# Carrying the odd head quads' outputs into the even quads' empty rows: an output projection of five matmuls per tile instead of eight

## The chip, the cores and the metric

The kernel runs on one core of one Trainium2 chip. The metric is the device time of one execution in microseconds (us). The profile is of one execution and reads the busy and waiting time of each engine: TensorE (PE, with its weight loads as PEld), VectorE (DVE), ScalarE (ACT), GpSimd (POOL) and SyncE (SP), whose queue here issues nearly all DMAs.

## The reference

A transformer block with adaptive layer norm, for 2048 tokens of width D = 512, in bfloat16. Cut to what matters:

```python
mod = silu(c) @ w_mod                      # six vectors of 512: sa, ca, ga, sb, cb, gb
h = layernorm(x) * (1 + ca) + sa
q, k, v = split(h @ wqkv)                  # 32 heads of 16 columns
o = softmax(q k^T / 4) v                   # per head, all 2048 keys
x = x + ga * (o @ wo)                      # the output projection that is changed
h = layernorm(x) * (1 + cb) + sb
x = x + gb * ((gelu(h @ w_gate) * (h @ w_up)) @ w_down)   # inner width 1792
```

The scores are 32 x 2048 x 2048 numbers, and each of them needs an exponential. Head h owns columns 16h to 16h + 15 of o, and so rows 16h to 16h + 15 of wo.

## The kernel before, in words

**Units and steps.** The queries are cut into six sets (`SETS`): three of 512, one of 256 and two of 128. A *unit* is one set with one *quad* of four heads. Eight quads cover the 32 heads: quad qd holds heads 8(qd//2) + 2j + (qd mod 2) for j = 0 to 3, so an even quad has the even heads of a group of eight and the following odd quad the odd ones. For the first four quads, the two sets of 128 are run as one unit of 256. A *step* of the main loop (`stream`, lines 1202 to 1453) is one group of score matmuls into three PSUM banks (ps_sc), and one ScalarE instruction that takes the exponentials of them. There are two such groups of banks, so the matmuls of a step wait until ScalarE is done with the step before the last. ScalarE writes 1536 columns (three banks) or 1024. Where it writes 1024, VectorE makes the third bank's exponentials by an integer trick: one tensor_scalar per bank out of PSUM (L338, into dreg or mreg), and after four of them four shifted copies (mreg<-dreg, mreg<-mreg).

**Output of a unit.** The value matmuls of a quad write four blocks of 17 rows into ps_pv, at partitions 0, 32, 64 and 96: sixteen rows of output and, as the seventeenth, the softmax's denominators. `unit_end` (lines 1506 to 1545) copies that to SBUF (osb), and sends the denominators through a chain of DMAs on SP's queue: osb to DRAM (`scr_den`), back as 128 partitions (`den`), a reciprocal on VectorE, to DRAM again (`scr_rec`), and four broadcasting loads into `rb`. Then `fin2` multiplies osb by rb on VectorE and writes `onorm[:, qd]`. Quads 6 and 7 of the last two sets take a shorter way (`near_end`, lines 934 to 949): a selecting matmul (osb,self) spreads the denominators and VectorE takes reciprocals of 128 x 128. In `onorm[:, qd]` sixteen of every 32 rows carry outputs; the others are zero or meet zero rows of the projection's weights.

**Output projection.** `side_wo` (lines 951 to 966) makes, for each tile of 128 queries, eight matmuls over 128 rows and 512 columns, one per quad (`wo_mm`). In the main loop each is issued as four instructions of 32 output rows (`mm` with `split`, lines 304 to 314), which run side by side. I call such a four a *group*. The weights `wo` are eight tiles, each zeroed first, with sixteen of every 32 rows loaded (`side_wo_load`) and multiplied by ga (`scale_wo`). The last set's projection is `wo_last`, with the eighth matmul in `tail_end`.

**What sets the order.** Nothing is scheduled while the kernel runs: a recorder writes each engine's list of instructions when the program is built. It holds a model of each engine's time and of DMA latencies, and at each point chooses between the next step's score matmuls, value matmuls, side work (the projections and the feed-forward part of an earlier set, `side_ffn`, given out by a credit against due positions in `plan`), and idle matmuls (`xs,ident`) that it adds where the last 3413 ns held fewer than `FILL` columns (`short`). VectorE, SP and some ScalarE work stands in a list of tasks, taken by `urgency` (lines 1083 to 1093). Each engine then runs its own list in order and waits on semaphores, so a late operand holds up everything behind it on that engine. After the last step, `tail` orders what is left: the last set's projection, its layer norm and feed-forward part.

Line 313 is `mm`'s matmul, 326 `act`, 330 `tt`, 338 `ts`, 343 `stt`, 347 `copy`, 350 `recip`, 376 the DMA, and `ps_mi` the PSUM bank of the side work.

Of the kernel before, what the change touches and what calls it, by code (L numbers as in the profile page):

```python
# [7 lines left out]
BF16 = mybir.dt.bfloat16  # L8
# [5 lines left out]
P = 128  # L14
S_TOK = 2048
D = 512
# [16 lines left out]
BCOL = (0, 0, 0, 0, 0, 128)  # L33
QS = 4
CH = 3
SC = 2 * CH
# [382 lines left out]
class _Kernel(_Recorder):  # L419
# [12 lines left out]
    def alloc(self):  # L432
# [31 lines left out]
        self.vs = sb("vs", [P, len(SHIFT), NKT - T0, H * VW], BF16)  # L464
        self.wo = sb("wo", [P, 8, D], BF16)
        self.E = sb("E", [P, NSL, 512], BF16)
# [368 lines left out]
    def side_wo_load(self):  # L835

        if not self.dry:
            self.task([lambda qd=qd: self.memset("dve", self.wo[:, qd, :], 0.0) for qd in range(8)]
                      + [lambda: self.memset("dve", self.self32[:, :], 0.0)], "wo0")
        yield from self.until("wo0")  # L840
        selv = self.self32[:, :].rearrange("p (a b) -> p a b", b=32)
        self.affine_select(selv, [[-32, 4], [0, 32]], ALU.not_equal, 1.0, -16, 1)
        for j in range(4):
            for ee in range(2):
                src = self.A_wo.rearrange("(a j e r) n -> j e r a n", j=4, e=2, r=DH)[j, ee]
                self.dma("sp", self.wo[32 * j:32 * j + DH, ee:8:2, :], src, "wo%d" % (2 * j + ee))
        yield END
# [22 lines left out]
    def scale_wo(self):  # L870

        if not self.dry:
            self.task([lambda qd=qd: self.tt("dve", self.wo[:, qd, :], self.wo[:, qd, :], self.ga[:, :], ALU.mult)
                       for qd in range(8)], "wo", self.after(["modB"]))
        return
        yield
# [3 lines left out]

    def wo_mm(self, bank, gi, tl, qd, first=True):
        c = OCOL[gi] + P * tl
        self.mm(bank, self.onorm[:, qd, c:c + P], self.wo[:, qd, :], start=first and qd == 0, stop=(qd == 7))

# [66 lines left out]
    def side_wo(self, gi):  # L951
        q0, W = SETS[gi]
        n = W // P
        tiles = [q0 // P + i for i in range(n)]
        mi = self.mi[:, :]
        for i in range(n):
            for qd in range(8):
                yield from self.until(("onorm", gi, qd))
                yield 512, lambda i=i, qd=qd: self.wo_mm(mi, gi, i, qd)
            self.wo_fin(mi, tiles[i])  # L960
            if not self.dry:
                self.task([lambda t=tiles[i]: self.ln_stat(t)], ("st2", tiles[i]))
# [120 lines left out]
    def urgency(self, tk):  # L1083

        if tk[1] is not None and tk[1][0] in ("rec", "onorm", "stats", "rstd") or tk[1] in ((("ln2", len(SETS) - 1, h) for h in range(2))):
            return -3
        if tk[1] is not None and tk[1][0] == "shift" and self.plain[tk[1][1]] <= LATE:
            return -2
        if tk[1] is None or tk[1][0] in ("st2", "ln2", "den"):
            return -1  # L1090
        if tk[1] is None or tk[1][0] != "shift":
            return 1
        return 0 if self.plain[tk[1][1]] <= URGENT else 2
# [412 lines left out]
    def unit_end(self, u, acc):  # L1506
# [25 lines left out]
        def fin2():  # L1532
            c = OCOL[sets[0]]
            self.tt("dve", self.onorm[:, qd, c:c + W], osb, rb, ALU.mult)
            if self.probing is None:
                self.live.pop(u)
                for k in sets:
                    self.done(("onorm", k, qd))
# [5 lines left out]
        self.task(steps, ("den", u))  # L1544
        self.task([fin2], None, free)

# [42 lines left out]
    def wo_last(self, k):  # L1589

        yield from self.until("last")
        yield from self.until("wo")
        yield 512, lambda: self.mm(self.spare[0], self.ident[:, :], self.xs[:, SETS[k][0] // P, :], start=True, stop=False)
        for qd in range(7):
            yield from self.until(("onorm", k, qd))
            yield 512, lambda qd=qd: self.wo_mm(self.spare[0], k, 0, qd, False)
        if not self.dry:
            self.done("wo_last")
        yield END

    def tail_end(self, k):
# [8 lines left out]
        yield from self.until(("onorm", k, 7))  # L1610
        yield lambda: self.wo_mm(bank, k, 0, 7, False)
        halves = [slice(0, D // 2), slice(D // 2, D)]
# [143 lines left out]
```

## Time and profile before

| what | before |
|---|---|
| median of 3 runs (range) | 859.36 us (859.06 to 859.92) |
| the profiled execution's own time | 860.08 us |
| its span, first to last instruction | 858.3 us |
| ScalarE busy | 831.8 us (97%) |
| TensorE busy | 797.3 us (93%) |
| VectorE busy | 700.3 us (82%) |
| projection matmuls in the main loop (ps_mi<-wo,onorm) | 480 instructions, 37.8 us busy |
| multiplications that write onorm | 44 |
| DMAs issued by SP | 401 |
| idle matmuls (xs,ident of 512 columns) | 396 instructions, 99 groups |

The busy time of an engine is the time in which at least one of its instructions ran. Instructions of one engine overlap, so the mean of one is longer than the distance from one start to the next. A line of waits names the engine that was idle, its tile and line, and what ended its idle time, with the sum, the number and the longest. In a line of the timeline the first number is the start, the second the length of a run of equal instructions, and a bracket gives the idle time just before and what ended it.

### The profile page before, as it was taken

The numbers are of one execution on the slowest core, as the hardware profiler recorded it, in microseconds if no ns is written. First come the engines' busy times: TensorE is split into PE (matmuls) and PEld (weight loads), VectorE is DVE, ScalarE is ACT, GpSimd is POOL, SyncE is SP. The second block draws the span as 40 slices with busy tenths as digits, with TensorE's granted clock in tenths as the row PEclk, the third lists the DMA queues.
The fourth block names the chain that finished last, engine by engine and source line by source line (L and its number), as shares of the span: only waits on it lengthen the run. The fifth ranks groups of instructions, "written<-read, shape, count | busy, mean of one in ns | idle before, by whom it ended". The sixth has DMA issues, their size and how long they took to land.

```text
span 858.3 us, 27911 instructions
## 1 busy us (share of the span) xinstructions
PE 797.3 (93%) x12580; PEld 288.0 (34%) x12582; DVE 700.3 (82%) x1351; ACT 831.8 (97%) x747; POOL 4.5 (1%) x12
## 2 busy tenths in 40 slices
PE   7889999999999899899999999999998999998998
PEld 3334332322222222222222222222343323345566
DVE  7865989989889989988898988989987764687575
ACT  6999999999999999999999999999999999999992
POOL 1000000000000000000000000000000000000000
PEclk9999999999999999999999999999999999999999
DMA  9000000000003111210002112120133222500000
GB/s 311 10 26 18 2 9 9 10 9 9 10 4 93 44 45 33 58 33 19 11 15 82 42 36 58 34 58 9 46 104 112 62 78 60 153 10 11 19 7 14
DMA packets 64233, 38.08 MB, mean 44 GB/s; under 512 B 17745, under 2 KB 61970, under 8 KB 64114
## 3 DMA queue, kind: packets, MB, share of 16 engines
q1 hardware_dynamic: 63056, 35.65, 14.7%
q8 instruction: 98, 1.61, 0.8%
q10 hardware_dynamic: 1058, 0.66, 0.3%
q14 instruction: 21, 0.17, 0.1%
HBM read 33.68 MB, written 2.61 MB: 42 GB/s over the span
## 4 chain that ended last, share of the span: by engine, by line
ACT 74%; PE 16%; DVE 7%; DMA 1%; issue 1%; SPq 0%; ACTq 0%; DVEq 0%
ACT E L326 72%; PE ps_mi L313 6%; PE ps_sc L313 6%; PE ps_pv L313 3%; ACT wreg L326 2%; DVE mreg L338 1%; DMA mreg<-in_w_mod_dram 1%; DVE st L366 1%; DVE wreg L343 1%; DVE hreg L338 1%; DVE wreg L347 1%; SPq L376 0%; DVE dreg L338 0%; DVE nwt L330 0%; DMA rb<-scr_rec 0%
## 5 line engine op out<-in xcount | busy, mean ns | idle before, releaser
L326 ACT ACTIVATE E<-ps_sc 128x1536 bf16<-128x1536 f32 (+2 forms) x698 | 804.1, 1339 | 11.6 <-PE ps_sc L313 11.0
L313 PE MATMUL ps_sc<-qT,kmo 32*128 32x512 bf16 (+2 forms) x1408 | 177.4, 323 | 10.1 <-ACT E L326 8.6
L313 PE MATMUL ps_sc<-qT,kme 32*128 32x512 bf16 (+2 forms) x1408 | 173.0, 323 | 12.7 <-ACT E L326 10.1
L313 PE MATMUL ps_pv<-E,vaug 128*17 128x512 bf16 (+2 forms) x2400 | 170.4, 318 | 2.4 <-DVE vaug L347 1.0
L338 DVE TENSOR_SCALAR dreg<-ps_sc 128x512 uint16<-128x512 f32 x196 | 135.1, 690 | 35.0 <-PE ps_sc L313 32.6
L338 DVE TENSOR_SCALAR mreg<-dreg 128x2048 uint16<-128x2048 uint16 x196 | 127.8, 681 | 0.4 <-PE ps_pv L313 0.4
L313 PE MATMUL ps_mi<-wreg,mreg 128*32 128x512 bf16 (+2 forms) x1504 | 110.2, 370 | 13.2 <-DVE wreg L343 6.8
L313 PE MATMUL ps_pv<-mreg,vs 128*17 128x512 bf16 (+2 forms) x1408 | 102.8, 344 | 2.1 <-DVE mreg L338 1.8
L313 PEld LDWEIGHTS ps_sc<-qT,kme 32*128 32x128 bf16 x1408 | 47.5, 91 | 130.5 <-ACT E L326 97.4
L313 PEld LDWEIGHTS ps_sc<-qT,kmo 32*128 32x128 bf16 x1408 | 47.6, 91 | 121.3 <-ACT E L326 93.6
L313 PEld LDWEIGHTS ps_pv<-E,vaug 128*17 128x17 bf16 x2400 | 53.5, 89 | 85.7 <-issue 58.2
L338 DVE TENSOR_SCALAR mreg<-ps_sc 128x512 uint16<-128x512 f32 x96 | 66.3, 691 | 16.8 <-PE ps_sc L313 15.0
L338 DVE TENSOR_SCALAR mreg<-mreg 128x2048 uint16<-128x2048 uint16 x96 | 62.9, 684 | 0.0
L313 PEld LDWEIGHTS ps_mi<-wreg,mreg 128*32 128x32 bf16 (+1 forms) x1504 | 34.1, 95 | 65.8 <-issue 20.4
L347 DVE CAST wreg<-ps_mi 128x512 bf16<-128x512 f32 x51 | 35.0, 686 | 18.2 <-PE ps_mi L313 17.7
L343 DVE SCALAR_TENSOR_TENSOR wreg<-wreg,ps_mi 128x512 bf16<-128x512 bf16 x51 | 34.9, 685 | 11.8 <-PE ps_mi L313 7.8
L313 PEld LDWEIGHTS ps_pv<-mreg,vs 128*17 128x17 bf16 x1408 | 31.6, 89 | 33.3 <-DVE mreg L338 16.8
L313 PE MATMUL ps_mi<-hreg,wreg 128*32 128x512 bf16 (+1 forms) x496 | 39.5, 377 | 1.9 <-DVE hreg L338 1.0
L313 PE MATMUL ps_mi<-wo,onorm 128*32 128x512 bf16 x480 | 37.8, 383 | 0.1
L330 DVE TENSOR_TENSOR wreg<-wreg 128x1024 bf16<-128x1024 bf16 (+1 forms) x60 | 35.9, 603 | 0.7
L330 DVE TENSOR_TENSOR onorm<-osb,rb 128x512 bf16<-128x512 f32 (+2 forms) x44 | 23.4, 536 | 11.7 <-DMA rb<-scr_rec 11.6
L313 PE MATMUL ps_mi<-mreg,hreg 128*32 128x512 bf16 x384 | 32.3, 384 | 0.0
(147 smaller groups left out, 566.0 us busy)
## 6 DMA issues: line engine op xcount, KB each, us to landing
mreg<-in_B_w_up_dram SPq DMA_DIRECT2D x25, 256.0 KB, 3.2
mreg<-in_B_w_gate_dram SPq DMA_DIRECT2D x21, 256.0 KB, 2.9
rb<-scr_rec SPq DMA_DIRECT2D x96, 32.0 KB, 1.8
mreg<-in_B_w_down_dram SPq DMA_DIRECT2D x12, 256.0 KB, 2.8
dreg<-in_B_w_down_dram SPq DMA_DIRECT2D x9, 256.0 KB, 3.0
mreg<-in_w_mod_dram SPq DMA_DIRECT2D x1, 2048.0 KB, 11.2
out_dram<-xs SPq DMA_DIRECT2D x15, 128.0 KB, 1.8
xs<-in_A_x_dram SPq DMA_DIRECT2D x3, 512.0 KB, 9.0
```

The lines of the kernel that those rows point to most:

```text
L313: return self.rec("pe", lambda e: e.matmul(out, lhsT, rhs, start=start, stop=stop, tile_position=tp), [lhsT, rhs], [out], cost=(n, int(rhs ...
L326: return self.rec("act", lambda e: e.activation(out, in_, func, scale=scale, **kw), rd, wr, cost=self.cost("act", out, [in_], "act"))
L330: return self.rec(eng, lambda e: e.tensor_tensor(out, a, b, op), [a, b], [out], cost=self.cost(eng, out, [a, b], "tt"))
L338: return self.rec(eng, lambda e: e.tensor_scalar(out, a, s1, s2, **kw), rd, [out], cost=self.cost(eng, out, [a], "ts") + (60 if len(rd) > ...
L343: return self.rec("dve", lambda e: e.scalar_tensor_tensor(out, a, s, b, op0=op0, op1=op1), rd, [out], cost=self.cost("dve", out, [a, b], " ...
L347: return self.rec(eng, lambda e: e.tensor_copy(out, in_), [in_], [out], cost=self.cost(eng, out, [in_], "ts"))
L366: return self.rec("dve", lambda e: e.bn_stats(out, in_), [in_], [out], cost=self.cost("dve", out, [in_], "bn"))
```

## The change

The sixteen output rows of an odd quad are copied into the sixteen empty rows of each 32 of the even quad before it. Two quads then stand in one tile of 128 rows, in the natural row order of wo, and share a matmul. For the first four sets the pairs are (0,1), (2,3) and (4,5), with 6 and 7 alone: five matmuls per tile. For the two sets of 128 the pairs are (0,1) and (2,3), with 4 to 7 alone: six matmuls.

- `wo` has seven tiles: three whole ones (one DMA), and four with sixteen of 32 rows for quads 4 to 7 (eight DMAs of half the size). Four tiles are zeroed instead of eight, seven are scaled instead of eight.
- After the multiplication of an odd quad of a pair, a new task `merge` issues four DMAs on SP's queue from SBUF to SBUF, one per head, of 16 rows by the set's width. The key that the projection waits for is set by the last of them.
- The tasks of the denominators (`den`) and of the multiplication (now keyed `norm`) move to the highest class of urgency, with which the recorder takes them ahead of other VectorE tasks.
- In `tail_end` the second half of the last transposes waits until the feed-forward part of the set before has left its PSUM bank.

```diff
+MERGED = (((0, 1), (2, 3), (4, 5), (6,), (7,)), ((0, 1), (2, 3), (4,), (5,), (6,), (7,)))
...
-        self.wo = sb("wo", [P, 8, D], BF16)
+        self.wo = sb("wo", [P, 7, D], BF16)
...
+        wov = self.A_wo.rearrange("(a p) n -> p a n", p=P)
+        self.dma("sp", self.wo[:, 0:3, :], wov[:, 0:3, :], "wo8")
         for j in range(4):
             for ee in range(2):
                 src = self.A_wo.rearrange("(a j e r) n -> j e r a n", j=4, e=2, r=DH)[j, ee]
-                self.dma("sp", self.wo[32 * j:32 * j + DH, ee:8:2, :], src, "wo%d" % (2 * j + ee))
+                self.dma("sp", self.wo[32 * j:32 * j + DH, 3 + ee:7:2, :], src[:, 2:4, :], "wo%d" % (2 * j + ee))
...
+    def merged(self, gi):
+        return MERGED[gi >= len(SETS) - 2]
+
+    def wo_mm(self, bank, gi, tl, g, first=True):
+        c, qd = OCOL[gi] + P * tl, g[0]
+        self.mm(bank, self.onorm[:, qd, c:c + P], self.wo[:, qd // 2 if len(g) == 2 else qd - 1, :],
+                start=first and qd == 0, stop=(qd == 7))
...
-            for qd in range(8):
-                yield from self.until(("onorm", gi, qd))
-                yield 512, lambda i=i, qd=qd: self.wo_mm(mi, gi, i, qd)
+            for g in self.merged(gi):
+                for qd in g:
+                    yield from self.until(("onorm", gi, qd))
+                yield 512, lambda i=i, g=g: self.wo_mm(mi, gi, i, g)
...
-        if tk[1] is not None and tk[1][0] in ("rec", "onorm", "stats", "rstd") or tk[1] in ((("ln2", len(SETS) - 1, h) for h in range(2))):
+        if tk[1] is not None and tk[1][0] in ("rec", "norm", "onorm", "stats", "rstd", "den") or tk[1] in ((("ln2", len(SETS) - 1, h) for h in range(2))):
             return -3
...
-        if tk[1] is None or tk[1][0] in ("st2", "ln2", "den"):
+        if tk[1] is None or tk[1][0] in ("st2", "ln2"):
             return -1
...
+        pair = (qd - 1, qd) in self.merged(sets[0])
...
+        def merge(j):
+            c = OCOL[sets[0]]
+            self.dma("sp", self.onorm[32 * j + DH:32 * j + 2 * DH, qd - 1, c:c + W], self.onorm[32 * j:32 * j + DH, qd, c:c + W],
+                     "de%d%d" % (qd // 2, j))
+            if self.probing is None and j == 3:
                 for k in sets:
                     self.done(("onorm", k, qd))
...
-        self.task([fin2], None, free)
+        self.task([fin2], ("norm", u), free)
+        if pair:
+            self.task([("sp", lambda j=j: merge(j)) for j in range(4)], None,
+                      self.after([("half", u)] + [("onorm", k, qd - 1) for k in sets]))
...
             yield from self.until(("ln2", k, h))
+            if h:
+                yield from self.until(("part", k - 1))
```

`wo_last` loops over the merged groups but the last in the same way, `scale_wo` over seven tiles, and `tail_end` calls `wo_mm` with the group (7,).

More of the change, by code (lines that the diff above doesn't have):

```diff
@@ L837, in side_wo_load @@
         if not self.dry:
-            self.task([lambda qd=qd: self.memset("dve", self.wo[:, qd, :], 0.0) for qd in range(8)]
+            self.task([lambda i=i: self.memset("dve", self.wo[:, i, :], 0.0) for i in range(3, 7)]
                       + [lambda: self.memset("dve", self.self32[:, :], 0.0)], "wo0")
@@ L873, in scale_wo @@
             self.task([lambda qd=qd: self.tt("dve", self.wo[:, qd, :], self.wo[:, qd, :], self.ga[:, :], ALU.mult)
-                       for qd in range(8)], "wo", self.after(["modB"]))
+                       for qd in range(7)], "wo", self.after(["modB"]))
         return
@@ L879, in normed @@
         return self.E[:, NSL - 1, :] if k == len(SETS) - 1 else self.tb2[:, i, :]
-    def wo_mm(self, bank, gi, tl, qd, first=True):
-        c = OCOL[gi] + P * tl
-        self.mm(bank, self.onorm[:, qd, c:c + P], self.wo[:, qd, :], start=first and qd == 0, stop=(qd == 7))
+    def merged(self, gi):
[4 more added lines that the diff above has]
+                start=first and qd == 0, stop=(qd == 7))
     def wo_fin(self, bank, t):
@@ L1536, in fin2 @@
                 self.live.pop(u)
+                self.done(("half", u))
+                if not pair:
+                    for k in sets:
+                        self.done(("onorm", k, qd))
+        def merge(j):
[3 more added lines that the diff above has]
+            if self.probing is None and j == 3:
                 for k in sets:
@@ L1593, in wo_last @@
         yield 512, lambda: self.mm(self.spare[0], self.ident[:, :], self.xs[:, SETS[k][0] // P, :], start=True, stop=False)
-        for qd in range(7):
-            yield from self.until(("onorm", k, qd))
-            yield 512, lambda qd=qd: self.wo_mm(self.spare[0], k, 0, qd, False)
+        for g in self.merged(k)[:-1]:
+            for qd in g:
+                yield from self.until(("onorm", k, qd))
+            yield 512, lambda g=g: self.wo_mm(self.spare[0], k, 0, g, False)
         if not self.dry:
@@ L1610, in tail_end @@
         yield from self.until(("onorm", k, 7))
-        yield lambda: self.wo_mm(bank, k, 0, 7, False)
+        yield lambda: self.wo_mm(bank, k, 0, (7,), False)
         halves = [slice(0, D // 2), slice(D // 2, D)]
```

## The prediction

> **What bounds the kernel now.** I read the page's shares first, then the chain of work that ended last, then ScalarE's own waits, and last the timeline at the places where ScalarE stood idle.
>
> ```profile
> PE 797.3 (93%) x12580; PEld 288.0 (34%) x12582; DVE 700.3 (82%) x1351; ACT 831.8 (97%) x747; POOL 4.5 (1%) x12
> ...
> ACT 74%; PE 16%; DVE 7%; DMA 1%; issue 1%; SPq 0%; ACTq 0%; DVEq 0%
> ...
> L313 PE MATMUL ps_mi<-wo,onorm 128*32 128x512 bf16 x480 | 37.8, 383 | 0.1
> ```
>
> ScalarE is busy 97% of the span of 858.3 us and holds 74% of the chain. The projection is 37.8 us of TensorE's 797.3. The stretches say where ScalarE's 26.5 us of idle time are (columns: busy us of PE, PEld, DVE, ACT, POOL):
>
> ```profile
> 0.00:44.00 44.00, 35.27 (x488) 15.51 (x488) 34.84 (x118) 35.44 (x39) 4.19 (x11) 1.00 0.49 157
> 44.00:836.00 792.00, 743.20 (x11834) 257.47 (x11837) 652.97 (x1203) 790.06 (x697) 0.31 (x1) 1.00 0.14 39
> ACT E L326 <- PE ps_sc L313: 2.1, 3, 0.9
> ```
>
> 8.6 us are the prologue, 1.9 us the 792 us of the main loop, and 16.0 us (26.5 - 8.6 - 1.9) come after its last exponential. The third line is ScalarE's waits from 44 to 823 us: three for scores. Idle time hides part of the loss, because an exponential of 1536 columns lasts 1.54 us and the next starts 1.33 us after it: each visible gap costs about 0.2 us more. Summed over the trace, starts from 44 us on stand 11 us later than the shortest distances (1.33 us for 1536 columns, 0.90 us for 1024) would put them. So 11 us is all that the loop could give.
>
> The two larger gaps. First, in the projection of the first set:
>
> ```profile
> 238.54 7.34 ACT L326 ACTIVATE E<-ps_sc 128x1536 bf16<-128x1536 f32 x6
> 246.47 2.37 ACT L326 ACTIVATE E<-ps_sc 128x1024 bf16<-128x1024 f32 x2 [0.58 <-PE ps_sc L313]
> 244.22 0.61 PE L313 MATMUL ps_pv<-mreg,vs 128*17 128x512 bf16 x8
> 244.84 1.05 PE L313 MATMUL ps_mi<-wo,onorm 128*32 128x512 bf16 x16
> 245.72 0.39 PE L313 MATMUL ps_pv<-E,vaug 128*17 128x512 bf16 x4
> 246.04 0.61 PE L313 MATMUL ps_sc<-qT,kmo 32*128 32x512 bf16 x6
> ```
>
> Seven groups (two value, four projection, one value) stand between two steps' scores, and ScalarE waits for the scores behind them. Four projection groups start 0.88 us before what follows: 0.22 us a group. Second, at the start of the third set's feed-forward part:
>
> ```profile
> 655.04 2.20 SPq L376 DMA_DIRECT2D dreg<-in_B_w_down_dram  x3
> ...
> 657.80 1.89 SPq L376 DMA_DIRECT2D rb<-scr_rec  x4
> 662.61 0.43 DVE L330 TENSOR_TENSOR onorm<-osb,rb 128x256 bf16<-128x256 f32 x1 [1.30 <-DMA rb<-scr_rec]
> 663.69 0.83 PE L313 MATMUL ps_mi<-wreg,mreg 128*32 128x512 bf16 x12 [1.56 <-DVE wreg L347]
> 664.89 2.79 ACT L326 ACTIVATE E<-ps_sc 128x1536 bf16<-128x1536 f32 x2 [0.85 <-PE ps_sc L313]
> ```
>
> The reciprocals are issued behind three weight loads, VectorE stands before the multiplication, the copy out of ps_mi behind it is late, TensorE stands with scores behind, and ScalarE loses 0.85 + 0.2 = 1.05 us.
>
> **The change part by part.** Where I say "order" I mean the instructions of the built programs, engine by engine.
>
> *ScalarE's work: 0.* In the order, its 372 exponentials of 1536 columns, 320 of 1024 and all else are as many as before. VectorE takes 73 quad-steps in both. So the time changes only by ScalarE's gaps.
>
> *TensorE's load: -7.7 us, off the path.* The projection goes from 120 groups in ps_mi to 76, and in the last set from five groups and three whole matmuls to four and two: 46 x 0.22 = 10.1 us less. The recorder adds 11 idle groups: 2.4 us more. In a loop where ScalarE is idle 1.9 us of 792 this is worth nothing by itself; if TensorE were the bound there, all 7.7 us would be gained. I take 0, and price the places.
>
> *First set's projection: -0.78 us.* In the order the longest run between scores there is now four groups (a value group and three of projection) where it was seven. The gap of 0.58 + 0.2 us goes.
>
> *The late reciprocals: -1.05 us.* In the order the four loads of rb now stand ahead of the three weight loads and behind two others. If they still land late, 0; I take the whole.
>
> *A new heavy step: +0.78 us.* Some 60 us before the end, the fourth set's down matmuls and value matmuls put eight groups of 0.22 us before a step, behind an exponential of 0.90 us. The nearest row is the gap at 246.47 (0.78); 0 if ScalarE has enough in hand, 1.0 with one group more than there.
>
> *Other heavy steps: 0.* Steps with six or more groups ahead of the scores are 14 before and 9 after; their price in the trace is mostly below 0.2 us. Without the two gaps above, 9.2 of the 11 us are left, spread over some 600 steps; I let a fifth go or come, -1.9 to +1.9.
>
> *The carries: 0.* 14 x 4 DMAs on SP's queue. An issue takes 0.34 to 0.74 us there (rb's fours: 1.71 to 2.95), so four take about 2 us, and landing 1.9 us by the rb rows of the same 16 KB. From a carry to the first projection matmul that needs it, the order has at least 18 us of exponentials: hidden. On SP's queue only two of the 14 stand inside the next unit's denominator chain. If that cover is gone, each delays that chain by its 2 us: +4.0 at most if VectorE and ScalarE pay for all of it; a gain is excluded, since the carries only add issues.
>
> *Weights of the projection: 0.* Four memsets of 272 ns and one scaling of 418 ns less on VectorE, one DMA more on SP; loads at 58 to 62 us, scaling from 84.9 us, first use at 235 us. ScalarE has no gap there to give or take. *Urgency: 0,* bounds as for the other heavy steps. The extra wait in the last transposes: 0, since in the order these stand behind the same matmuls as before.
>
> *After the last exponential: -0.93 us.* Before, the last scores start at 833.69, and then:
>
> ```profile
> 835.18 1.25 PE L313 MATMUL ps_sc<-wo,onorm 128*32 128x512 bf16 x20
> 836.37 0.90 PE L313 MATMUL ps_mi<-wreg,mreg 128*128 128x128 bf16 x13
> 837.20 0.62 PE L313 MATMUL ps_pv<-E,vaug 128*17 128x128 bf16 x32
> ...
> 840.71 0.38 PE L313 MATMUL ps_sc<-wo,onorm 128*128 128x512 bf16 x1
> ```
>
> In the new order, behind those scores (over at 834.0) come a value group (0.33), sixteen up matmuls (0.89), an idle group (0.3), three projection groups (0.66), a value group (0.33), a projection group (0.22) and the last value group: it starts at about 836.75 and ends by 837.1 instead of 837.75. Then come the copy of osb (0.29), the selecting matmul (0.4), the reciprocal (0.95) and the multiplication (0.29), without the two feed-forward products of VectorE that stood between them; they end at 839.4, and TensorE reaches the last projection matmul at 839.7. VectorE's last feed-forward product before the statistics then ends at 840.25, where the statistics start; before they started at 841.18. Bounds: 0 if it shifts nothing, -1.2 if TensorE's place didn't hold. From the statistics on both orders are the same.
>
> **Sum.** -0.78 - 1.05 + 0.78 - 0.93 = -1.98 us. The profiled execution (858.3 us of span, 1.8 around it) took 860.08 us, 0.72 above the median, so 858.1 for it and 857.4 for the median.
>
> [...]
>
> **Rivals.** *No gain to measure.* The gaps are chance meetings of a fixed order, and a new order has new ones. For it speaks that the load per step is much the same (57 steps take over 0.1 us more than the exponential before them, now 54), and that the work saved comes back in part as idle groups. Against it, the end's 0.93 us don't depend on that. It gives 858.4 with the end alone, 859.4 without.
>
> *Slower, by late reciprocals.* VectorE waits for rb six times (11.6 us, the longest 4.31, at 802.99), and at 662 us ScalarE paid 0.8 us for each us. With `den` and `norm` most urgent and a carry inside the chain, the multiplication of the two last sets' fourth quad stands in the order only 2.7 us behind its last rb issue. A wait of 4.31 plus the 0.68 of the copy behind it, paid in full, gives -1.98 + 5.0 = +3.0: 862.4. It decides from 3.7 us of such waits. Against it, the wait of 4.31 itself cost ScalarE next to nothing, with work in hand.
>
> [...]
>
> **How the numbers follow.** A measurement of this kernel can tell about 0.2% (1.7 us). Faster by more (below 857.6): 0.55. Within it: 0.31, the first rival. Slower (above 861.1): 0.14, the second. Down to 854.7: the forecast with 1.9 from the other steps and no new heavy step (-0.78). Up to 861.3: no gain at all, with +1.9 from the other steps; only the second rival lies beyond.
>
> **What would show it.** ScalarE busy 831 to 832 us with 692 large exponentials; TensorE near 790; ps_mi<-wo,onorm x304 at about 24 us; no gap above 0.3 us in the first set's projection or at the first wait for the third set's weights; one near the fourth set's last down matmuls; last statistics to span's end 17.1 us as now. Wrong: new gaps of over 1 us on ScalarE behind onorm<-osb,rb, or projection matmuls that wait for onorm.

## The result, and the profile after

The changed kernel took 862.85 us (median of 9 executions, 861.70 to 865.59), the kernel before beside it 859.39 us (9 executions, 858.92 to 861.35): a ratio of 1.0041, with a 95% interval of 1.0031 to 1.0052. That is 3.5 us slower, twice the bound that I set for "slower", where 857.4 us and "faster" were forecast. In some executions of every version the mean granted clock of TensorE was below 1.000 (0.994 to 1.000 in the nine of the changed kernel), which widens the ranges below; it is part of the finding, and comes back at the end.

From the page of the changed kernel, the busy times and the chain of work that ended last:

```profile
PE 788.1 (92%) x12491; PEld 283.9 (33%) x12493; DVE 698.1 (81%) x1346; ACT 833.4 (97%) x747; POOL 4.5 (1%) x12
...
ACT 65%; PE 16%; DVE 9%; DMA 6%; SPq 3%; issue 1%; DVEq 0%
```

TensorE is 9.2 us less busy than before (797.3). ScalarE's share of the chain fell from 74% to 65%; what took its place is DMA (1% before) and SyncE's queue (0%). The groups with their shapes kept apart, and the stretch of the main loop:

```profile
L314 PE MATMUL ps_mi<-wo,onorm 128*32 128x512 bf16 x304 | 25.4, 384 | 1.6 <-DVE rb L351 0.7 <-DVE xs L331 0.5 <-DVE wreg L331 0.3
```

```profile
44.00:836.00 792.00, 730.79 (x11652) 251.22 (x11640) 647.31 (x1187) 786.70 (x693) 0.31 (x1) 1.00 0.15 40
```

The projection fell from 37.8 to 25.4 us, as announced. But ScalarE now works 786.7 us of these 792, where it was 790.06: its idle time in the loop went from 1.9 to 5.3 us. The waits of the changed kernel (engine, tile, what ended them: sum, number, longest):

```profile
ACT E L327 <- PE ps_sc L314: 13.2, 22, 2.1
DVE onorm L331 <- DMA rb<-scr_rec: 12.7, 9, 3.6
...
DVE rden L351 <- DMA den<-scr_den: 4.5, 5, 2.2
...
PE ps_mi L314 <- DMA mreg<-in_B_w_gate_dram: 1.3, 1, 1.3
PE ps_mi L314 <- DMA mreg<-in_B_w_up_dram: 1.1, 1, 1.1
```

ScalarE waits for scores 22 times instead of 11. VectorE waits for `rb` 9 times (6 before) and for `den` 5 times, 4.5 us (once, 1.4 us, before); and TensorE waits twice for feed-forward weights, which it did not do before.

**Where the time went.** I took the distance from each ScalarE start to the next, less the short distance (the lowest tenth) of the same pair of kinds in these two traces, and summed the excess by stage of the span:

| stage, us | before | after | difference |
|---|---|---|---|
| 44 to 240 | 2.67 | 3.13 | +0.46 |
| 240 to 250 (first set's projection) | 0.82 | 0.10 | -0.72 |
| 250 to 640 | 4.92 | 6.02 | +1.10 |
| 640 to 700 (third set's feed-forward part starts) | 1.30 | 2.87 | +1.57 |
| 700 to 760 | 0.94 | 1.65 | +0.71 |
| 760 to 800 | 0.52 | 1.92 | +1.40 |
| 800 to the last exponential | 0.81 | 1.35 | +0.54 |
| sum | 11.98 | 17.05 | +5.07 |

The rest: the first 44 us ran 1.36 us faster, and the stretch from the last exponential to the span's end 0.94 us faster: 5.07 - 1.36 - 0.94 = 2.77, the difference of the spans (861.1 against 858.3). The 1.36 us are not the change's: two later executions of lists that are the same up to there (e17, e18 below) were also 1.2 to 1.3 us earlier at 44 us than the profiled execution of the kernel before. Nor are the 0.46 us of the first stage: e4, e17 and e18, which share that kernel's lists for TensorE and ScalarE up to there, lose 0.5 to 0.6 us at 82 us just as the changed kernel does.

Three places in the timeline of the changed kernel (start, length, engine, what; in the bracket the idle time before and what ended it). The start of the third set's feed-forward part:

```profile
656.23 0.20 DVE L351 RECIPROCAL rden<-den 128x8 f32<-128x8 f32 x1 [0.70 <-DMA den<-scr_den]
656.35 1.33 DVE L339 TENSOR_SCALAR hreg<-xs,mv,rstd 128x512 bf16<-128x512 bf16 x4
656.46 0.34 SPq L377 DMA_DIRECT2D scr_rec<-rden  x1
656.77 1.42 PE L318 MATMUL ps_mi<-ident,hreg 128*128 128x128 bf16 x8 [0.42 <-DVE hreg L339]
656.84 0.44 SPq L377 DMA_DIRECT2D mreg<-in_B_w_gate_dram  x1
...
658.57 1.45 ACT L327 ACTIVATE E<-ps_sc 128x1536 bf16<-128x1536 f32 x1 [0.53 <-PE ps_sc L314]
...
659.80 1.45 SPq L377 DMA_DIRECT2D dreg<-in_B_w_down_dram  x3
...
661.29 0.47 SPq L377 DMA_DIRECT2D mreg<-in_B_w_gate_dram  x1
...
667.29 1.05 PE L314 MATMUL ps_mi<-wreg,mreg 128*32 128x512 bf16 x16 [1.31 <-DMA mreg<-in_B_w_gate_dram]
...
672.40 1.45 ACT L327 ACTIVATE E<-ps_sc 128x1536 bf16<-128x1536 f32 x1 [0.40 <-PE ps_sc L314]
```

The reciprocal `rden<-den`, now in the highest class, stands in VectorE's list ahead of the third set's four normalisations and waits 0.70 us for its DMA; these, TensorE's transposes and then ScalarE are late by 0.42 and 0.53 us. In the kernel before it stood behind them and did not wait:

```profile
653.13 1.38 DVE L338 TENSOR_SCALAR hreg<-xs,mv,rstd 128x512 bf16<-128x512 bf16 x4
...
654.43 0.20 DVE L350 RECIPROCAL rden<-den 128x8 f32<-128x8 f32 x1
```

On SyncE's queue the three `dreg` loads, which had made `rb` late, now stand behind it and just ahead of the second gate load. That load is issued at 661.29 (657.28 before) and lands at 667.16, 5.9 us later, and TensorE waits 1.31 us for it at 667.29. The first gate load is also issued later, at 656.84 instead of 651.43, behind the write of the reciprocal, but it lands at 659.82, in time. The wait for `rb` that cost 1.05 us here before is gone; two others have its place.

The fourth set's down matmuls, where I had expected a heavy step:

```profile
795.10 0.83 PE L314 MATMUL ps_mi<-xs,hreg 128*32 128x512 bf16 x12
795.75 0.40 PE L314 MATMUL ps_pv<-mreg,vs 128*17 128x128 bf16 x16
795.98 0.60 PE L314 MATMUL ps_mi<-xs,hreg 128*32 128x512 bf16 x8
...
796.41 0.39 PE L314 MATMUL ps_mi<-hreg 128*32 128x512 bf16 x4
...
796.62 0.40 PE L314 MATMUL ps_pv<-E,vaug 128*17 128x128 bf16 x16
796.95 0.62 PE L314 MATMUL ps_sc<-qT,kmo 32*128 32x128 bf16 x24
797.39 3.28 ACT L327 ACTIVATE E<-ps_sc 128x1024 bf16<-128x1024 f32 x3 [0.70 <-PE ps_sc L314]
```

Eight groups (six of down matmuls, two of value matmuls) stand ahead of the scores at 796.95, 64 us before the end, and ScalarE waits 0.70 us. Last, the end:

```profile
838.61 1.46 ACT L327 ACTIVATE E<-ps_sc 128x1536 bf16<-128x1536 f32 x1
...
843.30 0.38 PE L314 MATMUL ps_sc<-wo,onorm 128*128 128x512 bf16 x1
...
843.95 0.69 DVE L367 BATCH_NORM_STATS2 st<-ps_sc 128x6 f32<-128x512 f32 x1
```

From the last exponential to the statistics it takes 5.34 us (838.61 to 843.95), where it took 6.28 (834.90 to 841.18).

### The profile page after: what moved, and what is told of

It reads as the page before. It is cut to its first block, busy times and chain, and to the rows that moved or that the text cites. A ratio compares the mean times of both kernels' runs of the same rounds, so it can differ in the third digit from the quotient of the medians.

```text
span 861.1 us, 27809 instructions
## 1 busy us (share of the span) xinstructions
PE 788.1 (92%) x12491; PEld 283.9 (33%) x12493; DVE 698.1 (81%) x1346; ACT 833.4 (97%) x747; POOL 4.5 (1%) x12
## 4 chain that ended last, share of the span: by engine, by line
ACT 65%; PE 16%; DVE 9%; DMA 6%; SPq 3%; issue 1%; DVEq 0%
ACT E L327 63%; PE ps_mi L314 8%; PE ps_sc L314 5%; SPq L377 3%; PE ps_pv L314 2%; DMA rb<-scr_rec 2%; ACT wreg L327 2%; DMA scr_rec<-rden 1%; DVE wreg L344 1%; DVE st L367 1%; DVE wreg L348 1%; DMA den<-scr_den 1%; DMA mreg<-in_B_w_gate_dram 1%; DVE hreg L339 1%; DVE dreg L339 1%
## 5 line engine op out<-in xcount | busy, mean ns | idle before, releaser
L314 PE MATMUL ps_sc<-qT,kmo 32*128 32x512 bf16 (+2 forms) x1408 | 182.1, 323 | 11.1 <-ACT E L327 9.1
L314 PE MATMUL ps_sc<-qT,kme 32*128 32x512 bf16 (+2 forms) x1408 | 176.5, 323 | 16.5 <-ACT E L327 13.4
L314 PEld LDWEIGHTS ps_sc<-qT,kmo 32*128 32x128 bf16 x1408 | 50.2, 91 | 122.3 <-ACT E L327 93.1
L339 DVE TENSOR_SCALAR mreg<-ps_sc 128x512 uint16<-128x512 f32 x96 | 66.2, 690 | 18.2 <-PE ps_sc L314 17.2
L327 ACT ACTIVATE wreg<-wreg 128x1024 bf16<-128x1024 bf16 (+1 forms) x30 | 29.8, 1007 | 0.1
```

The costliest lines, as they stand in the source:

```text
L314: return self.rec("pe", lambda e: e.matmul(out, lhsT, rhs, start=start, stop=stop, tile_position=tp), [lhsT, rhs], [out], cost=(n, int(rhs ...
L327: return self.rec("act", lambda e: e.activation(out, in_, func, scale=scale, **kw), rd, wr, cost=self.cost("act", out, [in_], "act"))
L339: return self.rec(eng, lambda e: e.tensor_scalar(out, a, s1, s2, **kw), rd, [out], cost=self.cost(eng, out, [a], "ts") + (60 if len(rd) > ...
```

## The experiments

Each was timed beside the kernel before on the same chip, which took 859.7 to 860.7 us (medians of 11 to 23 executions). Five names for theories appear in the expectations: U (the new urgency), C (the carries), O (the order of the lists, whatever the work), Q (SyncE's queue), E (large transfers ahead of small ones make these late, whichever queue issues them) and W (the new work itself).

**Urgency.** e1 is the changed kernel with the old classes, e2 the kernel before with the new ones:

```diff
-        if tk[1] is not None and tk[1][0] in ("rec", "norm", "onorm", "stats", "rstd", "den") or tk[1] in (...):
+        if tk[1] is not None and tk[1][0] in ("rec", "onorm", "stats", "rstd") or tk[1] in (...):
...
-        if tk[1] is None or tk[1][0] in ("st2", "ln2"):
+        if tk[1] is None or tk[1][0] in ("st2", "ln2", "den", "norm"):
```

> The changed kernel with the tasks of the denominators and of the multiplication by the reciprocals back in their old class of urgency; carries and five matmuls stay. Theory U (urgency: the more urgent reciprocals and multiplications stand in VectorE's list ahead of DMAs that have not landed, and their DMAs stand on SP's queue ahead of weight loads): about 859 us, most of the 3.5 us back. Theory O (order: before's list happens to be a good one, and every new list of the same rules loses 2 to 5 us): 861 to 864 us. Theory C (carries: the 56 DMAs on SP's queue make what stands behind them late): 862 to 863 us.

> The kernel before with the new urgency alone: no carries, eight matmuls per tile. Theory U: 861.5 to 863 us, the loss of the change. Theory C: 859 to 860 us. Theory O: its lists differ from before's in few places (121 lines of TensorE's order), so little: 859 to 861 us.

e1 took 872.74 us (ratio 1.0148, 1.0131 to 1.0165), e2 859.97 us (1.0003, 0.9992 to 1.0014). So the new urgency is not the loss: alone it costs nothing that can be told, and without it the merged version is 10 us worse. U falls.

**Carries.** e4 adds unused carries to the kernel before; e8 lets GpSimd issue those of the changed kernel. TensorE's and ScalarE's lists are those of the version changed.

```diff
+            def carry(j):
+                self.dma("sp", self.onorm[32 * j + DH:32 * j + 2 * DH, qd - 1, c:c + W], self.onorm[32 * j:32 * j + DH, qd, c:c + W],
+                         "de%d%d" % (qd // 2, j))
+            self.task([("sp", lambda j=j: carry(j)) for j in range(4)], None,
+                      self.after([("onorm", k, x) for k in sets for x in (qd - 1, qd)]))
```

> The kernel before with the 14 carries of four DMAs added on SP's queue, and the projection still in eight matmuls (the carried rows meet zero weights). TensorE's and ScalarE's lists are the same as before. Theory C: 861.5 to 863 us. Theories U and O: 859 to 860 us.

> The changed kernel with all lists as they are, but with its 56 carries issued by GpSimd instead of SyncE. Theory Q: the carries' share of the queue (four issues of about 0.6 us ahead of the load of the up weights that landed at 715 us and held TensorE for 1.1 us) goes: 861-862, half of what moving the weight loads gives. Theory E and theory O: 862-864, no change.

e4 took 861.14 us (1.0016, 1.0000 to 1.0032), e8 863.07 us (1.0035, 1.0022 to 1.0048). The carries alone cost 1.4 us at the edge of what can be told; e4's four executions at a mean clock of 1.000 took 859.97 to 861.33 us, where the kernel before took 859.7 at that clock (median of 52). It makes no difference that can be told to the changed kernel which queue issues them. They are at most a part.

**TensorE's saved work.** e17 leaves the projection matmuls that the change merges away out of the kernel before, with all lists and waits as they were:

```diff
+        self.skipping = qd in ((1, 3, 5) if gi < len(SETS) - 2 else (1, 3))
         self.mm(bank, self.onorm[:, qd, c:c + P], self.wo[:, qd, :], start=first and qd == 0, stop=(qd == 7))
+        self.skipping = False
...
         for op in self.ops:
+            if op.skip:
+                left.update({s: max(n, left.get(s, 0)) for s, n in op.waits.items()})
+                continue
```

> The kernel before with all lists and waits as they are, but without the projection matmuls of the odd quads that the change merges away (1, 3 and 5 of the first four sets, 1 and 3 of the last two); their part of the output is left out, so this prices only the matmuls. TensorE busy falls by about 9 us. Prediction's step (off the path): within 0.5 us of the kernel before except for the gap of 0.78 us in the first set's projection: 858.9-859.7. If TensorE were the bound: 851-853. If fewer columns lower the clock somewhere: 860-862.

It took 859.96 us (1.0006, 0.9988 to 1.0024), 0.3 us above the range expected, with 182 TensorE instructions fewer and TensorE busy 791.6 us instead of 797.3, so 5.7 us less where 9 were expected. In the order of the kernel before, the work that the change saves is worth nothing that can be told: the seven executions at a mean clock of 1.000 took 859.4 us in the median, 0.3 us less than those of the kernel before.

**Large loads ahead of small ones.** e3 is the kernel before with `FILL = 4300`, so the same work in another order. It lost 3.6 us at the third set's start. In e9 the lists are those of e3, but on SyncE's queue the third set's three `dreg` loads stand 14 issues later; e10 does this in the changed kernel (10 issues), e18 in the kernel before (15).

```diff
-                self.dma("sp", self.wdst[i], v[:, 2 * i:2 * i + 2, :], "sd%d" % i)
+                self.dma("sp", self.wdst[i], v[:, 2 * i:2 * i + 2, :], "sd%d" % i, via="later" if i < 3 and gi == 2 else None)
...
+            if op.eng == "later":
+                late.append((len(prog["sp"]) + LATER, run))
+                continue
```

> The kernel before with 4300 instead of 4200 columns as the floor under which idle matmuls are added: the work is the same but for some idle matmuls, while nearly the whole order of TensorE, VectorE and ScalarE comes out anew. Theory O: 861 to 865 us, as much slower as the change. Theories U and C: 859 to 860 us, since urgency and carries are untouched.

> The kernel before with the idle-matmul bound at 4300 (864.5 us), all lists as they are, but in SyncE's list the third set's three dreg weight loads stand behind the reciprocals of that unit and the next (14 issues later, still 40 us before their first use). Theory E (large loads ahead of small ones): the four loads of rb lose 768 KB of the 1.5 MB ahead of them, VectorE's wait of 3.20 us at 665 falls below 1 us, ScalarE's loss of 3.5 us at 663 and the lower clock behind it go: 860.5-861.5. Theory O (any list loses by its own chance meetings): another place pays, 863-865.

> The changed kernel with all lists as they are, but with the third set's three dreg weight loads 10 issues later on SyncE's queue, behind the rb loads at 671. Theory E: the gate load that landed 5.86 us after its issue lands some 2 us earlier, TensorE's wait of 1.31 us at 667.3 goes, and with it what ScalarE loses at 668 to 673 (0.9 us): 861.5-862.3. If the loss is spread over all of 650 to 840 us (theory O): 862.4-863.2.

> The kernel before with all lists as they are, but with the third set's three dreg weight loads behind the next two units' rb loads on SyncE's queue, as in e9. Theory E and the prediction's step of the late reciprocals: VectorE's wait of 1.30 us at 662.61 and ScalarE's loss of 1.05 us go, nothing else changes: 858.4-859.2, just below the kernel before. Theory O, or another transfer that is late in its place: 859.5-861.

e3 took 864.54 us (1.0061, 1.0042 to 1.0081), e9 862.97 (1.0029, 1.0016 to 1.0042), e10 863.58 (1.0037, 1.0025 to 1.0049), e18 859.34 (0.9992, 0.9981 to 1.0003). The timeline of e3:

```profile
656.68 2.67 SPq L376 DMA_DIRECT2D dreg<-in_B_w_down_dram  x3
...
659.90 1.89 SPq L376 DMA_DIRECT2D rb<-scr_rec  x4
...
664.78 0.42 DVE L330 TENSOR_TENSOR onorm<-osb,rb 128x256 bf16<-128x256 f32 x1 [3.20 <-DMA rb<-scr_rec]
...
665.87 1.90 PE L313 MATMUL ps_mi<-wreg,mreg 128*32 128x512 bf16 x16 [2.57 <-DVE wreg L347]
668.36 1.45 ACT L326 ACTIVATE E<-ps_sc 128x1536 bf16<-128x1536 f32 x1 [3.15 <-PE ps_sc L313]
```

and of e9, where the loads stand behind the two units' `rb`:

```profile
654.28 12.39 ACT L328 ACTIVATE E<-ps_sc 128x1536 bf16<-128x1536 f32 x9
...
662.32 0.43 DVE L332 TENSOR_TENSOR onorm<-osb,rb 128x256 bf16<-128x256 f32 x1 [0.62 <-DMA rb<-scr_rec]
```

VectorE's wait fell from 3.20 to 0.62 us, and ScalarE's gap of 3.15 us went: in the table's measure e3 lost 3.64 us from 640 to 700, e9 0.39. The chain from weight loads over `rb`, VectorE and TensorE to ScalarE is shown. But e9's median gained only 1.6 us: in its profiled execution another wait for `rb` (1.67 us at 760.07) cost ScalarE 1.68 us, in the same list that had paid 0.9 us there in e3. e18 shows the price that the prediction gave this place:

```profile
653.81 12.30 ACT L328 ACTIVATE E<-ps_sc 128x1536 bf16<-128x1536 f32 x9
...
660.61 0.41 DVE L332 TENSOR_TENSOR onorm<-osb,rb 128x256 bf16<-128x256 f32 x1
```

No wait for `rb`, no gap; against the trace of the kernel before, ScalarE's lead grew by 1.10 us between 642 and 677 us and stayed to the end. The medians differ by 0.6 us, which this measurement can't tell from none. In e10, too, the place improved:

```profile
660.79 0.43 SPq L379 DMA_DIRECT2D mreg<-in_B_w_gate_dram  x1
...
666.91 1.05 PE L316 MATMUL ps_mi<-wreg,mreg 128*32 128x512 bf16 x16
...
669.99 4.19 ACT L329 ACTIVATE E<-ps_sc 128x1536 bf16<-128x1536 f32 x3
```

The second gate load landed 3.0 us after its issue instead of 5.9, TensorE no longer waited for it, ScalarE's gap of 0.40 us went, and the stretch from 640 to 700 us lost 1.90 us instead of 2.87. So these loads made that gate load late. (It was issued at 661.29, not at 656.84 as the expectation of e5 below has it.) But the median gained nothing: 250 to 640 us lost 0.5 us more than in the trace of the changed kernel and 760 to 800 us 0.4 us more, with the same lists.

**The loads on another queue.** e5 (changed kernel), e6 (before) and e7 (e3's order) let GpSimd issue 63 feed-forward loads (the 51 of the expectation is a miscount), with `via="pool"` at the calls that load `wst` and `wdst`.

> The changed kernel with every engine's list as it is, but with the feed-forward weight loads (gate, up and down, 51 DMAs) issued by GpSimd instead of SyncE. Theory Q (SyncE's queue): the loss after 650 us comes from one queue in which the weight loads, the denominators' chain and the carries hold each other up. Then the gate load that was issued at 656.84 and landed at 667.15 goes out some 5 us earlier, TensorE's waits for weights (1.3 and 1.1 us) go, VectorE's waits for rb and den fall from 17 to below 10 us, and the time falls from 862.9 to 859.5-860.5. Theory E (the 16 DMA engines): what is late is late because the transfers share the engines; another queue changes nothing: 862-864. Theory O (nothing but the order of the lists): the lists are the same, so at most 1 us is gained: 862-863.

> The kernel before with the same loads on GpSimd's queue and all lists as they are. Theory Q: its one large gap (0.85 us at 664.89, behind rb) goes and nothing else: 858.5-859.5. Theory E: no change, 859-860; or more, if rb (issued by SyncE at the same moments) now shares the engines with loads that earlier stood behind it: up to 862. Theory O: 859-860.

> The kernel before with the idle-matmul bound at 4300 instead of 4200 (864.5 us, with a loss of 3.5 us at 663 us behind rb, and then a stretch of lower clock), and the feed-forward weight loads on GpSimd's queue. Theory Q: the 3.5 us and the fall of the clock behind them go: 860-861. Theory E: rb is as late as before, 864-865. Theory O: 864-865, since the lists are the same.

All lost: 872.06 (1.0137, 1.0122 to 1.0151), 870.51 (1.0122, 1.0109 to 1.0135) and 872.41 us (1.0144, 1.0130 to 1.0158). The timeline of e6 at the second set's end shows the largest of the new gaps:

```profile
629.92 2.31 POOL L377 DMA_DIRECT2D dreg<-in_B_w_down_dram  x3
...
630.49 2.17 SPq L377 DMA_DIRECT2D rb<-scr_rec  x4
...
637.76 0.69 DVE L331 TENSOR_TENSOR onorm<-osb,rb 128x512 bf16<-128x512 f32 x1 [3.44 <-DMA rb<-scr_rec]
638.50 0.40 PE L314 MATMUL ps_mi<-wo,onorm 128*32 128x512 bf16 x4 [2.75 <-DVE onorm L331]
...
639.73 1.45 ACT L327 ACTIVATE E<-ps_sc 128x1536 bf16<-128x1536 f32 x1 [2.97 <-PE ps_sc L314]
```

SyncE issues `rb` from 630.49, without a load of its own in front, but GpSimd began to issue 768 KB 0.6 us earlier, behind two other weight loads. VectorE starts on `rb` 5.1 us after the last of its issues is over (632.66, 637.76), where such loads land 1.8 us after their issue in the median. Here separate queues did not keep small transfers from large ones; in e9 and e18 one queue in a better order did. Q's forecasts fail. Weight loads of GpSimd also landed later (5.2 us median for `dreg` in e6, 3.0 from SyncE in the kernel before), which is a second reason for the loss that these runs don't separate; a queue of another engine was not tried.

**More orders.** The model's landing of DMAs was made later, in both kernels, or the bound of idle matmuls was raised in the changed one:

```diff
-            op.t1 = self.dma_free + (1000 if run > 64 else 1500)
+            op.t1 = self.dma_free + (2500 if run > 64 else 3000)
```

(1700 and 2200 in e14 and e15; `FILL = 4300` in e13 and e16.)

> The changed kernel recorded with a model in which a DMA's result is there 2.5 (small rows 3.0) us after its bytes have moved instead of 1.0 (1.5), so that VectorE's list has more work ahead of each onorm<-osb,rb and each rden<-den; work and operations as in the changed kernel, another order. Theory E (VectorE waits in order for late small transfers): waits for rb and den fall from 17 us to below 6, 859-861. Theory O: a new order like any other, 860-866.

> The kernel before recorded with the same later landing of DMAs, so another order of the same work. Theory E: waits for rb fall from 11.6 us to below 5, the gap at 664.89 goes: 858-860, and below the changed kernel with the same model only by what the carries cost. Theory O: 860-866, since the list of the kernel before is better than the others of its kind by chance.

> The changed kernel with the idle-matmul bound at 4300 instead of 4200: the same work in another order, as e3 was of the kernel before. Theory O (the order decides, the change is worth about nothing): anywhere in 860 to 870. Theory W (the new work itself costs 3 us by its carries and its queue): 863 or more in every order, e3's 864.5 plus 3 in the mean.

> The changed kernel recorded with DMA results 1.7 (2.2) us after their bytes instead of 1.0 (1.5). Theory O: 860 to 870; waits of VectorE for rb and den between those of the changed kernel (17 us) and of e11 (2 us). Theory W: not below 862.

> The kernel before recorded with the same 1.7 (2.2) us. Theory O: 861 to 870, no better than e14 beyond their scatter. Theory W: some 3 us below e14, and near the 859.7 of the kernel before.

> e11 with the idle-matmul bound at 4300. e11 stood at 862.4 with mean clocks of 0.992 to 0.996; over all runs so far a clock lower by 0.001 goes with 0.63 us, so that without dips e11 would stand at about 859.5. If the dips come from stretches with too few columns, 4300 takes some away: 859.5 to 861.5. If they come from waits behind other engines, it is one more order: 861 to 868.

All orders side by side (us; in brackets the ratio's interval):

| rules of the recorder | old work | new work |
|---|---|---|
| old urgency, FILL 4200, landing 1.0/1.5 | before: 859.4 to 860.7 | e1: 872.7 (1.0131 to 1.0165) |
| new urgency | e2: 860.0 (0.9992 to 1.0014) | changed kernel: 862.9 (1.0031 to 1.0052) |
| FILL 4300 (old urgency for old work) | e3: 864.5 (1.0042 to 1.0081) | e13: 871.3 (1.0098 to 1.0162) |
| landing 1.7/2.2 (the same) | e15: 868.4 (1.0070 to 1.0106) | e14: 863.3 (1.0024 to 1.0050) |
| landing 2.5/3.0 (the same) | e12: 868.4 (1.0074 to 1.0129) | e11: 862.4 (1.0018 to 1.0041) |
| landing 2.5/3.0, FILL 4300 | not run | e16: 869.7 (1.0089 to 1.0126) |

The same work, but for the number of idle matmuls, moves by 9 to 10 us with its order, the old as the new. In rows 2 to 5 the new work is slower by 2.9 and 6.8 us and faster by 5.2 and 6.0: W, in its strong form of 3 us in every order, falls with these last two pairs (e14 against e15, e11 against e12). Theory O did not bound the spread well either: e1, e12, e13 and e16 came out above its ranges, by 1.3 to 8.7 us. What the change costs in the mean over orders stays open: the means of the columns are 864.2 and 867.0, with scatters of over 4 us. In the order of the kernel before, the saved matmuls came to 0.0 us (e17) and the carries to 1.4 (e4); if the parts add, some 2 of the 3.5 us came with the new order, an estimate that is good to a microsecond or two. No version beat the kernel before beyond what can be told; e18 comes nearest.

e11 also shows that VectorE's waits are not the measure. From its waits:

```profile
ACT E L327 <- PE ps_sc L314: 12.2, 12, 2.1
...
DVE rden L351 <- DMA den<-scr_den: 1.8, 1, 1.8
...
DVE onorm L331 <- DMA rb<-scr_rec: 0.8, 1, 0.8
```

VectorE waits 2.6 us for these DMAs, where it waited 17.2 in the changed kernel, and from 640 to 700 us e11 lost 0.42 instead of 2.87 us. Yet it took 862.39 us: other losses came (in the table's measure 1.15 us at 221, 1.15 at 416, 1.04 at 745), and its clock fell twice (a mean of 0.83 from 740 to 750 us and from 840 to 850). The stretch after the last exponential, too, is written anew with every order: 22.5 us in the changed kernel, 23.4 before, 24.1 in e13, 30.8 in e15 and 32.1 in e1, which lost most of its 13 us there.

## Why the prediction was wrong

*First set's projection, -0.78:* right in size. From 240 to 250 us the excess fell by 0.72 us and ScalarE is busy without a gap. But it is not shown that fewer groups did it. With the lists of the kernel before and the merged groups left out (e17), 0.53 of the 0.75 us that ScalarE lost at this gap stayed; and in e3, e12 and e15, with all eight matmuls in another order, no start in this projection is over 0.2 us late.

*A new heavy step, +0.78:* right, in place and size: eight groups, a gap of 0.70 us, 0.82 us from start to start.

*After the last exponential, -0.93:* right: 5.34 us to the statistics instead of 6.28, so -0.94, and 17.2 us from there to the end, as before. The way there fits too: counted from the last exponential, TensorE reaches the last projection matmul 0.1 us earlier than the working has it.

*TensorE's load, off the path:* right, and shown by itself in e17: leaving the merged matmuls out gave nothing that can be told. So the reading taken from ScalarE's 97%, that TensorE's load is off the path, held for the work saved. It does not say that a change of order is free.

*The late reciprocals, -1.05:* the mechanism and the price were right (e9 and e18: 1.10 us of ScalarE's lead in the order of the kernel before). The step failed in taking the place as empty afterwards. The wait for `rb` went, and the stretch from 640 to 700 us lost 1.57 us more than before: the three weight loads, now behind `rb`, made the gate load behind them late (0.97 us less is lost where they go later, e10), and VectorE waits for a `den` ahead of the normalisations. I had priced the new order of that queue for `rb` alone, not for what now stood behind those loads.

*Urgency, 0:* right as a sum (e2: 0.3 us above the kernel before, not to be told from 0), wrong for this order: the 0.70 us wait of `rden` at 656.23 cost ScalarE 0.71 us from start to start. With the old classes on the new work (e1) and with the new ones on the old work (e2) this reciprocal stands behind the normalisations and does not wait, so it takes both together.

*The carries, 0:* within its bounds of 0 to +4.0; e4 says about 1.4, barely measurable. The rows taken for them were near: an issue took 0.59 us in the median (0.54 to 1.58), so four 2.4 us instead of 2, and the landing 1.8 us instead of 1.9.

*Other heavy steps, 0, from -1.9 to +1.9:* this is the term that was mis-sized. Without the four places above and the first stage's 0.46 us, which are not the change's, the table's stages rose by 1.10 + 0.71 + (1.40 - 0.82) + 0.54 = 2.9 us, in many losses none of which is over 0.7 us. I had let a fifth of 9.2 us go or come. The bound should have come from how far a new order moves the same work: 4.8 us in e3, 8.7 in e12 and e15. Nothing in the one trace of before showed that; my reading of it gave the two known gaps that a new order would remove, but not those that it would bring. Counting steps with six or more groups (14, then 9) could not show them, since they come from late operands in a fixed order as much as from load: ahead of ScalarE's gap at 688.40 TensorE waits 0.94 us for VectorE, ahead of the one at 718.29 1.11 us for an up load.

So the sum: predicted for the loop -1.05, measured +5.07 (4.6 without the 0.46); for the end -0.93, measured -0.94. The first rival had the mechanism ("chance meetings of a fixed order, and a new order has new ones") and put it at nothing; its sign and its size were what was missing. The second rival came close in its time (862.4) but not by its mechanism: the long wait for `rb` that it named did not decide, the longest (3.57 us, at 741.07) cost ScalarE 0.2 to 0.3 us, and the gaps of over 1 us that were to show it are not there in this trace. The mechanism itself is real: in the profiled execution of e8, where only the issuer of the carries differs, the wait at that same multiplication was longer, and ScalarE lost 2.90 us behind it, TensorE's slower matmuls from 745 us on included (sixteen take 1.78 us at 745.05, and 1.05 us at 740.64):

```profile
743.97 0.42 DVE L332 TENSOR_TENSOR onorm<-osb,rb 128x256 bf16<-128x256 f32 x1 [5.75 <-DMA rb<-scr_rec]
...
747.84 1.45 ACT L328 ACTIVATE E<-ps_sc 128x1536 bf16<-128x1536 f32 x1 [2.90 <-PE ps_sc L315]
```

## What to carry to other kernels

Here, with the order written out ahead and ScalarE 97% busy, a local saving on TensorE (5.7 us of its busy time in e17) was worth only the gaps it closed, while a new order put every gap up for a new draw (4.8 us in e3, 8.7 in e12 and e15). Before forecasting a change to such a kernel, find that spread with a few orders of the unchanged work (another bound, another latency in the model), and read a result within it as the order's and not the change's. To see what an edit itself is worth, keep the lists and change one thing in them, as e17 and e18 do: 46 groups of matmuls were worth nothing that could be told, three loads moved on a queue 1.1 us of ScalarE's time in the trace, though the median can't show it.

## What the runs showed of the hardware

*A short wait of TensorE, and a longer stretch at half clock behind it.* In the traces the granted clock falls to 0.50 and comes back. Worked out from the mean clock of the stretches, it stood there for about 3.4 us in e3 (0.66 from 665 to 670 us), 6.8 in e15 (0.67 and 0.99 in the 10 us from 820 and from 830), 10.2 in e13 (0.50 and 0.99 in those from 810 and from 820), and 17 in e4 (0.71, 0.50, 0.50 and 0.59 in the four of 5 us from 805 to 825) and e12. In the 3.41 us before such a fall in the main loop (the reach of `short`) TensorE had been idle for 0.6 us (e17: 2.77 busy from 736.69 to 740.10) to 2.7 us (e6, in the gap that ends at 638.50). The stretches of e12 (busy us of PE, PEld, DVE, ACT, POOL, then the clock):

```profile
435.00:440.00 5.00, 4.02 (x47) 0.97 (x43) 4.78 (x9) 5.00 (x6) 0.00 (x0) 1.00 0.00 0
440.00:445.00 5.00, 4.61 (x33) 0.81 (x37) 3.02 (x6) 4.51 (x5) 0.00 (x0) 0.62 0.02 3
445.00:450.00 5.00, 5.00 (x37) 0.88 (x29) 2.66 (x5) 2.46 (x3) 0.00 (x0) 0.50 0.01 3
450.00:455.00 5.00, 5.00 (x36) 0.83 (x37) 2.61 (x5) 3.76 (x4) 0.00 (x0) 0.50 0.00 0
```

About 1 us of idle time from 435 to 440 us is followed by 17 us at half clock, in which TensorE is busy all the time and ScalarE is not: 8 us of excess for ScalarE from 425 to 475 us. But idle time alone does not decide it. In the kernel before, TensorE was idle for 1.55 of the following 3.41 us, and the clock stayed at 1.00 in the whole trace:

```profile
660.27:663.68 3.41, 1.86 (x36) 0.56 (x30) 1.89 (x5) 3.41 (x3) 0.00 (x0) 1.00 0.26 74
```

What does decide is not shown: a fall came after 0.6 us of idle time in e17 and none after these 1.55 us, and in e12 the clock stayed at 0.50 from 445 to 455 us, which the records show as busy throughout. Within the versions, over 232 executions, 0.001 less in the mean clock goes with 0.64 us more; so, as an estimate from these, 3.4 us at half, which takes 0.002 off the mean clock of the span, goes with 1.3 us, what the waits around it cost included. It explains a part of the loss only: the two executions of the changed kernel at a mean clock of 1.000 took 861.70 and 862.85 us, the 52 of the kernel before (beside e1 to e18) 859.7 in the median.

*A small load's landing.* In the kernel before, the loads of `rb` land 1.8 us (32 KB) and 1.9 us (16 KB) after their issue in the median; the four issued from 657.80 us, behind four weight loads of 256 KB, took 3.7. From the end of the last issue to VectorE's start it took 3.0 us in e3 (661.79, 664.78), where the same queue had issued 768 KB of weights from 656.68 on and 256 KB at 659.39, and 5.1 us in e6 (632.66, 637.76), where another queue had issued 768 KB from 629.92 on. Even with only an output write of 128 KB just ahead it differs: it took 1.3 us in the changed kernel (issued to 739.73, used at 741.07) and 3.3 us at the same place of e8 (740.66, 743.97), with the same lists but for the issuer of the carries; what held the last load there is not shown.
